# A first product by seven products in place of eight, with its sums formed in two PSUM banks

## The chip, the cores and the metric

One core of a Trainium2 chip runs one program. The metric is the time of one execution on the device in microseconds; the median of several runs is compared. The engines are named as the profile names them: PE is TensorE (PEld its weight loads), DVE is VectorE, ACT is ScalarE, POOL is GpSimd, and SP is SyncE, which issues most DMAs.

## The reference, cut to what matters

With S = 2048 rows, D = 576 columns and 4608 hidden features:

```
xn = layernorm(q)                                  # over the 576 columns
ks = causal convolution of k over 4 rows, per column
y  = causal convolution of (ks * v) over all 2048 rows, per column, by FFT
     + ks * v * ssm_D
h  = max(xn @ w1, 0)                               # 2048 x 576 by 576 x 4608: "first product"
out = q + xn * y + h @ w2                          # 2048 x 4608 by 4608 x 576: "second product"
```

All of it is in float32. The kernel keeps that precision on TensorE by splitting each operand into a high and a low part in the type fp32r and adding three matmuls (high by high, high by low, low by high); the product of two low parts is left out.

## The kernel before, in words

The 2048 rows are 16 tiles of 128, or 4 blocks of 512 rows (`BT` = 4 tiles each). The blocks are done in two halves of two blocks, because the running sums `acc` of one half (8 tiles of 576 columns) fill the space there is. In each half the 4608 features go by in 12 chunks of 384 (`FT` = 3 feature tiles of 128).

For a chunk and a block, `mm1` (L324 to L342) computes each feature tile transposed, 128 features by 512 rows, in one PSUM bank of the pool `ps_h` (2 banks): the 576 columns of x are four contraction tiles of 128 with three matmuls each (`h1` by `hi`, `h1` by `lo`, `l1` by `hi`), and a fifth of 64, whose high and low part lie stacked in one tile (`hl`), with two. That is 14 matmuls of 512 columns at L334. ScalarE then writes the high part `hh` of the relu (L339) and VectorE the low part `ll` (L340); both read the bank, and the bank is free after them. Those are the weights of the second product: `mm2` (L346 to L380) makes 128 rows by 288 columns in a bank of `ps_o` (3 banks) with 3 feature tiles x 3 = 9 matmuls of 288 columns (L358), and VectorE adds it to `acc` (L362 for the first block, which still multiplies by `rstd`, L366 for the others).

The weights arrive by DMA on SP (`load_w1`, L282; `load_w2`, L294). ScalarE makes the high part (`h` at L306 and L315) and GpSimd subtracts for the low part (`split_lo`, L277). `first_xT` (L211) and `make_xT` (L246) normalise a block's rows, transpose them on TensorE (L234, L269) and split them (`xhi` at L203 on ScalarE, `xlo` at L204 on VectorE). Blocks 2 and 3 are made so at the end of the first half.

The long convolution is a second stream of work, the generator `conv` (L410 to L714), in four stages: `fk` transforms the kernel `ssm_k` (loaded as `kt`, L421), `fx` forms and transforms `ks * v` (matmuls at L398), `fm` multiplies in the transformed domain (matmuls at L562, with most of ScalarE's work), and `fo` transforms back (L700, L701). Its matmuls are 128 x 288 and go to three further banks, `ps_f`. `tick` (L726) decides when the stream's next step is issued: each piece of the feed-forward part passes its cost in matmul columns, a rate turns it into credit, and one step is taken when there is credit. Steps have weights `W_FK`, `W_FX`, `W_FM`, `W_FO` (L54), and a step may ask for a pause. `here` (L402) queues a step's ScalarE and VectorE instructions behind the latest relu and the latest addition to `acc`. The tool that builds the program orders each engine's queue by a model of the time line; on the chip each queue runs in that order.

Of the kernel before, what the change touches and what calls it, by code (L numbers as in the profile page):

```python
# [17 lines left out]
P = 128  # L18
# [8 lines left out]
FT = 3  # L27
FC = FT * P
NCHUNK = DFF // FC
# [15 lines left out]
W_MM1 = 14 * 512  # L45
W_MM2 = FT * 6 * NH
PAUSE = 16000
START = 4000
PAUSES = 16
SHARE = 0.985  # L50
# [3 lines left out]
W_FK, W_FX, W_FM, W_FO = 1.4, 4.1, 1.26, 2.4  # L54
KD = 36
KT_GAP = 6000
FFT_TOTAL = N_FK * W_FK + N_FX * W_FX + N_FM * W_FM + N_FO * W_FO

SPLITS = {(0, 1): ((1, 0),), (0, 2): ((1, 1),), (1, 0): ((1, 2), (2, 0)), (1, 1): ((2, 1),),
          (1, 2): ((2, 2),)}  # L60
SPLITS0 = {(1, 0): ((1, 0), (1, 1)), (1, 1): ((1, 2), (2, 0)), (1, 2): ((2, 1), (2, 2))}
FFN_TOTAL = NCHUNK * NB * (FT * W_MM1 + BT * W_MM2)


# [44 lines left out]
def h3_ffn_kernel(ctx: ExitStack, tc, x, k, v, shift_k, ssm_k, ssm_D, w1, w2, fwd, inv, mid, out):  # L109
# [8 lines left out]
    hp = ctx.enter_context(tc.tile_pool(name="hp", bufs=2 * FT))  # L118
    xp = ctx.enter_context(tc.tile_pool(name="xp", bufs=2))
    dram = ctx.enter_context(tc.tile_pool(name="dram", bufs=1, space=DRAM))  # L120
    ps_h = ctx.enter_context(tc.tile_pool(name="ps_h", bufs=2, space=PSUM))
# [11 lines left out]
    fin = dram.tile([HT // 2, P, 2, D], F32, name="fin")  # L133

# [21 lines left out]
    def load_x(t, tag, bufs, **queues):  # L156
        pair = xp.tile([P, 2, D], F32, tag=tag, name=f"{tag}{t}", bufs=bufs)
        move(pair, x, slice(t, t + 2), **queues)
        return pair

    def load_acc(t, **queues):
        pairs[t] = load_x(t, "acc", HT // 2, **queues)
        acc[t], acc[t + 1] = pairs[t][:, 0, :], pairs[t][:, 1, :]
# [27 lines left out]
    xT = {}  # L191
    done = {}

    def xT_tiles(b):
        hi = xp.tile([P, 4, 512], F32R, tag="xhi", name=f"xhi{b}")
        lo = xp.tile([P, 4, 512], F32R, tag="xlo", name=f"xlo{b}")
        hl = xp.tile([P, 512], F32R, tag="xhl", name=f"xhl{b}")
        xT[b] = (hi, lo, hl)

    def split_x(b, c, ps):  # L200
        hi, lo, hl = xT[b]
        if c < 4:
            last = nc.scalar.activation(hi[:, c, :], ps, AF.Copy)  # L203
            nc.vector.tensor_tensor(lo[:, c, :], ps, hi[:, c, :], OP.subtract)  # L204
            return last
        else:
            done["act"] = nc.scalar.activation(hl[:64, :], ps[:64, :], AF.Copy)
            done["dve"] = nc.vector.tensor_tensor(hl[64:, :], ps[:64, :], hl[:64, :],
                                                  OP.subtract)

    def first_xT(srcs):  # L211

        xT_tiles(0)
# [3 lines left out]
        neg = xp.tile([P, BT], F32, tag="neg", name="neg", bufs=1)  # L217
        behind = None
        for t in range(BT):
            if t % 2 == 0:  # L220
                pair = xp.tile([P, 2, D], F32, tag="xn", name=f"xn{t}", bufs=BT // 2)
# [14 lines left out]
        for c in range(5):  # L236
            last = split_x(0, c, ps[c])
            if c == 1:
                with tc.issue_after(last.ins):
                    split_w1(0, 1)  # L240
# [5 lines left out]
    def make_xT(b, srcs, in_place=False):  # L246

        xT_tiles(b)
        t0 = b * BT
        for t in range(t0, t0 + BT):  # L250
            at = done["acc"] if in_place else lows[2 * (t - t0) // BT]
            with tc.issue_after(at.ins):
                stats(t, srcs[t])
        with tc.issue_after(at.ins):
            inv_std(t0, BT)
        xn = []
        for t in range(t0, t0 + BT):
            if in_place:
                xn.append(srcs[t])
            else:  # L260
                if t % 2 == 0:
                    pair = xp.tile([P, 2, D], F32, tag="xn", name=f"xn{t}", bufs=BT // 2)
                xn.append(pair[:, t % 2, :])
            normalized(xn[-1], srcs[t], t)
        for c in range(5):
            w = min(P, D - c * P)
            ps = fft_psum()
            for i in range(BT):
                nc.tensor.transpose(ps[:w, i * P:(i + 1) * P], xn[i][:, c * P:c * P + w], ident)  # L269
            split_x(b, c, ps)  # L270

    def at_turn(ci):

        return tc.issue_after(done["act"].ins) if ci else nullcontext()
# [7 lines left out]
    def load_w1(ci):  # L282
        f0 = (ci % NCHUNK) * FC
        r1 = wp.tile([P, 5, FC], F32, tag="r1", name=f"r1_{ci}", bufs=1)
        for o, step in ((0, P), (P, FC - P)) if ci == 0 else ((0, FC),):
            f, to = slice(f0 + o, f0 + o + step), slice(o, o + step)
            queue = nc.gpsimd if step == P else nc.sync
# [3 lines left out]
        raw_w[1, ci] = r1  # L291
        weights[ci] = [[None, None, None, None] for _ in range(FT)]

    def load_w2(ci):  # L294
        f0 = (ci % NCHUNK) * FC
        r2 = wp.tile([P, FT, D], F32, tag="r2", name=f"r2_{ci}", bufs=1)
        nc.sync.dma_start(r2, w2[f0:f0 + FC, :].rearrange("(j p) d -> p j d", p=P))
        raw_w[2, ci] = r2

    def split_w1(ci, j):  # L300
        r1 = raw_w[1, ci]
        h1 = wp.tile([P, 5, P], F32R, tag="h1", name=f"h1_{ci}_{j}", bufs=2 * FT - 1)
        l1 = wp.tile([P, 5, P], F32R, tag="l1", name=f"l1_{ci}_{j}", bufs=2 * FT - 1)
        cols = slice(j * P, (j + 1) * P)
        with at_turn(ci):
            nc.scalar.activation(h1, r1[:, :, cols], AF.Copy)  # L306
# [538 lines left out]
```

## Time and profile before

| what | value |
|---|---|
| runs | 1083.4, 1084.87, 1086.86 us; median 1084.87 us |
| profiled execution: span from first to last instruction | 1084.4 us |
| mean granted TensorE clock in it | 0.997 |
| DMA | 150.79 MB, 139 GB/s on average |
| TensorE idle before its own instructions, longest cases | 2.51 us at 56.69 us; 2.22 us at 12.07 us |
| POOL's wait for ScalarE's high parts at L277 | 448.3 us for w1, 168.8 us for w2 |

The profile gives the profiled execution by its span; it has no other time of its own. A busy share is the time in which at least one instruction of an engine is recorded as running. Matmuls are pipelined and their ends are modelled, so TensorE's pace is read from the chain of waits in order of time, where a piece lasts until the next begins. In the groups, the number behind the first bar is the busy time in us and the mean ns of one; behind the second bar stands the idle time of the engine just before these instructions and who ended it.

### The profile page before, as it was taken

The numbers are of one execution on the slowest core, as the hardware profiler recorded it, in microseconds if no ns is written. First come the engines' busy times: TensorE is split into PE (matmuls) and PEld (weight loads), VectorE is DVE, ScalarE is ACT, GpSimd is POOL, SyncE is SP. The second block draws the span as 40 slices with busy tenths as digits, with TensorE's granted clock in tenths as the row PEclk, the third lists the DMA queues.
The fourth block names the chain that finished last, engine by engine and source line by source line (L and its number), as shares of the span: only waits on it lengthen the run. The fifth ranks groups of instructions, "written<-read, shape, count | busy, mean of one in ns | idle before, by whom it ended". The sixth has DMA issues, their size and how long they took to land.

```text
span 1084.4 us, 17301 instructions
## 1 busy us (share of the span) xinstructions
PE 1070.8 (99%) x6537; PEld 977.2 (90%) x6537; DVE 732.5 (68%) x1213; ACT 585.0 (54%) x1184; POOL 261.9 (24%) x218
## 2 busy tenths in 40 slices
PE   8999999999999999999999999999999999999998
PEld 5889899998999999999999999899999999999998
DVE  5423677949998777677666676666656666876774
ACT  4221587823443323333388787888788864543430
POOL 4131222412312322312213031211113032332410
PEclk9999999999999999999999999999999999999999
DMA  9950345664644525325564343434344227745524
GB/s 217 181 145 27 119 147 190 195 185 133 187 138 136 153 77 164 117 60 171 190 182 135 99 135 99 135 99 136 92 143 141 80 103 221 201 130 143 164 81 110
DMA packets 112255, 150.79 MB, mean 139 GB/s; under 512 B 45261, under 2 KB 62927, under 8 KB 112172
## 3 DMA queue, kind: packets, MB, share of 16 engines
q1 hardware_dynamic: 103884, 135.50, 42.0%
q0 software_dynamic: 7968, 13.44, 4.8%
q8 instruction: 52, 0.85, 0.3%
q10 hardware_dynamic: 320, 0.74, 0.3%
q14 instruction: 31, 0.25, 0.1%
HBM read 114.26 MB, written 35.39 MB: 138 GB/s over the span
## 4 chain that ended last, share of the span: by engine, by line
PE 90%; DMA 4%; SPq 2%; DVE 2%; ACT 1%; issue 1%; POOL 0%; ACTq 0%; DVEq 0%
PE pso L358 40%; PE psh L334 39%; PE psf L562 7%; PE psf L398 3%; DMA r<-in_w 3%; SPq L421 2%; PE psf L700 1%; PE psf L701 1%; DMA k-1_2414<-in_k 1%; DMA sk<-in_shift_k 0%; PE psf L269 0%; DVE lok L553 0%; POOL l L277 0%; DVE k L611 0%; DVE lox L553 0%
## 5 line engine op out<-in xcount | busy, mean ns | idle before, releaser
L277 POOL TENSOR_TENSOR l<-r,h 128x640 fp32r<-128x640 f32 (+1 forms) x144 | 224.4, 1563 | 621.8 <-ACT h L306 448.3
L358 PE MATMUL pso<-h,hh 128*128 128x288 f32 x1152 | 337.3, 295 | 3.7 <-ACT hh L339 2.7
L358 PE MATMUL pso<-l,hh 128*128 128x288 f32 x1152 | 338.5, 295 | 0.0
L358 PE MATMUL pso<-h,ll 128*128 128x288 f32 x1152 | 337.7, 295 | 0.0
L334 PE MATMUL psh<-xhi,h 128*128 128x512 f32 x576 | 226.5, 394 | 1.1 <-DVE ll L340 1.1
L334 PE MATMUL psh<-xlo,h 128*128 128x512 f32 x576 | 226.5, 393 | 0.0
L334 PE MATMUL psh<-xhi,l 128*128 128x512 f32 x576 | 225.8, 392 | 0.0
L358 PEld LDWEIGHTS pso<-h,hh 128*128 128x128 f32 x1152 | 215.8, 188 | 10.4 <-ACT hh L339 3.4
L358 PEld LDWEIGHTS pso<-l,hh 128*128 128x128 f32 x1152 | 216.3, 188 | 5.8
L358 PEld LDWEIGHTS pso<-h,ll 128*128 128x128 f32 x1152 | 216.0, 188 | 0.6
L366 DVE TENSOR_TENSOR acc<-pso,acc 128x288 f32<-128x288 f32 x288 | 128.6, 451 | 75.1 <-PE pso L358 72.1
L339 ACT ACTIVATE hh<-psh 128x512 fp32r<-128x512 f32 x144 | 85.6, 595 | 169.1 <-PE psh L334 168.2
L340 DVE SCALAR_TENSOR_TENSOR ll<-psh,hh 128x512 fp32r<-128x512 f32 x144 | 99.0, 687 | 109.8 <-ACT hh L339 109.5
L334 PEld LDWEIGHTS psh<-xhi,l 128*128 128x128 f32 x576 | 108.4, 188 | 20.3
L334 PEld LDWEIGHTS psh<-xhi,h 128*128 128x128 f32 x576 | 108.4, 188 | 17.1 <-DVE ll L340 1.4
L334 PEld LDWEIGHTS psh<-xlo,h 128*128 128x128 f32 x576 | 108.6, 188 | 15.5 <-DVE xlo L204 0.4
L315 ACT ACTIVATE h<-r 128x576 fp32r<-128x576 f32 x72 | 48.9, 682 | 73.4 <-DMA r<-in_w 46.9
L362 DVE SCALAR_TENSOR_TENSOR acc<-pso,rstd,acc 128x288 f32<-128x288 f32 x96 | 48.3, 512 | 27.5 <-PE pso L358 26.5
L392 DVE TENSOR_TENSOR ks<-kt,ks 64x288 fp32r<-64x288 f32 x64 | 57.6, 901 | 3.3 <-ACT ks L391 1.3
L399 ACT ACTIVATE zx<-psf 128x288 f32<-128x288 f32 x64 | 25.8, 407 | 59.3 <-PE psf L398 38.9
L334 PE MATMUL psh<-xhl,l 128*128 128x512 f32 x144 | 56.4, 392 | 0.0
L334 PE MATMUL psh<-xhl,h 128*128 128x512 f32 x144 | 56.2, 391 | 0.0
(109 smaller groups left out, 1451.2 us busy)
## 6 DMA issues: line engine op xcount, KB each, us to landing
r<-in_w SPq DMA_DIRECT2D x24, 864.0 KB, 5.3
r<-in_w SPq DMA_DIRECT2D x23, 768.0 KB, 6.1
zk<-zk SPq DMA_DIRECT2D x32, 288.0 KB, 2.5
zx<-zx SPq DMA_DIRECT2D x32, 288.0 KB, 2.6
ztk<-zk SPq DMA_DIRECT2D x32, 288.0 KB, 3.0
ztx<-zx SPq DMA_DIRECT2D x32, 288.0 KB, 2.8
zy<-vo SPq DMA_DIRECT2D x32, 288.0 KB, 2.1
zo<-zy SPq DMA_DIRECT2D x32, 288.0 KB, 3.0
```

Source lines behind the costliest of these rows:

```text
L277: return nc.gpsimd.tensor_tensor(dst, src, hi, OP.subtract)
L315: nc.scalar.activation(h2, r2[:, j, :], AF.Copy)
L334: nc.tensor.matmul(ps, a, m, start=i == 0, stop=i == len(seq) - 1)
L339: done["act"] = nc.scalar.activation(hh, ps, AF.Relu)
L340: lows.append(nc.vector.scalar_tensor_tensor(ll, ps, 0.0, hh, op0=OP.max, op1=OP.subtract))
L358: nc.tensor.matmul(ps[:, :NH], a[:, cols], m[:, dc], start=n == 0, stop=n == 3 * FT - 1)
L362: done["acc"] = nc.vector.scalar_tensor_tensor(acc[t][:, dc], ps[:, :NH], rstd[:, t:t + 1], acc[t][:, dc], op0=OP.mult, op1=OP.add)
L366: done["acc"] = nc.vector.tensor_tensor(acc[t][:, dc], ps[:, :NH], acc[t][:, dc], OP.add)
L392: nc.vector.tensor_tensor(dst[other], src[own], dst[own], OP.subtract)
L398: nc.tensor.matmul(ps[:, :NH], w[:, u, n, :], stk, start=n == 0, stop=n == 1)
L399: nc.scalar.activation(z, ps[:, :NH], AF.Copy)
L562: nc.tensor.matmul(ps[:, :NH], a, m[:, cols], start=n == 0, stop=n == 2)
```

## The change

**Feature tiles and work.** `FT` becomes 2; a "pair" n is 256 features, and there are 18 pairs in a half. The list `visits` goes through pairs and blocks so that the block visited last for one pair is visited first for the next (blocks s = 0, 1, then 1, 0, ...).

**The first product.** From the third pair on (68 of 72 visits) `quad` takes the place of `mm1`. It treats the two feature tiles, the four full contraction tiles (taken two and two) and the two row halves of the block (`HR` = 256 rows) as 2 x 2 matrices and makes the four results by 7 products in place of 8, each of 2 contraction tiles x 3 = 6 matmuls of 256 columns. The fifth contraction tile stays as it was (`rest`, 2 matmuls of 512 columns a feature tile). The pool `ps_h` still has two banks, now as `h0` and `h1`; the sums of products are formed in them by further matmuls, by two ScalarE copies (`m5`, and one from bank to bank) and by two VectorE adds that read a bank and `m5` and write a bank.

**The sums of operands.** GpSimd makes four sums of w1 tiles a pair (`sum_w`), and `split_group` splits the sums and the plain tiles, 2048 columns and the fifth tile's 256 a pair where 1280 were split. For the rows, `sums` makes `t1` to `t4` of a block on VectorE and splits them. All block sums are made before the convolution begins: those of blocks 0 and 1 (`keep_first`) during the third and fourth visit, those of blocks 2 and 3 (`later_xT`) during the first `quad` visits, stored in DRAM (`kept`) and loaded again (`fetch`) at the last pair of the first half.

**The second product.** Its work is cut into units of one row tile and 288 columns (`unit`), for the two pairs that a block has seen last, 12 matmuls a bank (6 where a block starts or ends with one pair). `fill` issues units worth two pairs after each of the four stages of a `quad`.

**The convolution.** Its stream starts after the block sums; constants come one tile at a time with 3 buffers; some tiles have fewer buffers; step weights become 1.73, 3.5, 1.94 and 2.2, the pause between pieces of `kt` 3000 columns in place of 6000, and the share of the feed-forward work over which it is spread 0.96 in place of 0.985.

```diff
-FT = 3
+FT = 2
+HR = 256
...
-W_FK, W_FX, W_FM, W_FO = 1.4, 4.1, 1.26, 2.4
+W_FK, W_FX, W_FM, W_FO = 1.73, 3.5, 1.94, 2.2
...
-KT_GAP = 6000
+KT_GAP = 3000
...
+    kept = dram.tile([HB, P, 4 * 7 * HR + 512], F32, name="kept")
...
+        with here():
+            tt(v[:, 0], b12, b11, OP.subtract)
+            split("t1", 0)
+        yield
+        with here():
+            tt(v[:, 2], high[:, :, b22], b12, OP.subtract)
+            tt(v[:, 2], low[:, :, b22], v[:, 2], OP.add)
+        yield
...
+    def sum_w(n, k):
...
+        dst, a, b, op = ((s13[:, :, left], one[:, :, right], two[:, :, right], OP.add),
+                         (s24[:, :, left], s13[:, :, left], one[:, :, left], OP.subtract),
+                         (s13[:, :, right], one[:, :, left], one[:, :, right], OP.subtract),
+                         (s24[:, :, right], two[:, :, left], s24[:, :, left], OP.subtract))[k]
+        nc.gpsimd.tensor_tensor(dst, a, b, op)
...
+    def product(n, s, a, b):
+        hi, lo = weights[n][a]
...
+        for kp in range(2):
+            seq += [(hi[:, kp], m[:, 0, kp]), (hi[:, kp], m[:, 1, kp]), (lo[:, kp], m[:, 0, kp])]
+        return seq
+
+    def quad(n, s, m):
+
+        first, other = slice(0, HR), slice(HR, 512)
+        pb, pa = bank(m, f"psb{n}_{s}"), bank(1 - m, f"psa{n}_{s}")
+        run_seq(pb[:, other], product(n, s, "s1", "t1"), True)
+        run_seq(pb[:, first], product(n, s, "a11", "b11"))
+        m5 = xp.tile([P, HR], F32, tag="m5", name=f"m5_{n}_{s}", bufs=1)
+        nc.scalar.activation(m5, pb[:, other], AF.Copy)
+        done["act"] = nc.scalar.activation(pa[:, first], pb[:, first], AF.Copy)
+        yield
+        run_seq(pa[:, first], product(n, s, "a12", "b21"))
+        run_seq(pb[:, first], product(n, s, "s2", "t2"))
+        nc.vector.tensor_tensor(pa[:, other], pb[:, first], m5, OP.add)
+        yield
+        run_seq(pb[:, first], product(n, s, "s3", "t3"))
+        nc.vector.tensor_tensor(pb[:, other], pb[:, first], m5, OP.add)
+        run_seq(pa[:, other], product(n, s, "s4", "b22"))
+        run_seq(pa, rest(n, 0, s))
+        relu(n, s, 0, pa)
+        yield
+        run_seq(pb[:, first], product(n, s, "a22", "t4"))
+        run_seq(pb, rest(n, 1, s))
+        relu(n, s, 1, pb)
+        yield
...
+    def fill():
+        room = 2
+        while work and work[0][0] <= room:
+            size, args = work.pop(0)
+            unit(*args)
+            room -= size
...
+            parts = quad(n, s, q % 2)
+            for st in range(4):
+                next(parts)
+                if n + 1 < HALVES * NPAIR:
+                    if second:
+                        split_group(n + 1, st)
+                        if st == 3 and n + 2 < HALVES * NPAIR:
+                            load_w1(n + 2)
+                    else:
+                        sum_w(n + 1, st)
+                if st == 1:
+                    split_w2(n, second)
+                    if n + 1 < HALVES * NPAIR:
+                        load_w2(n + 1, second)
...
+                tick(W_STAGE[st])
+                fill()
+                if n == NPAIR - 1:
+                    fetch(s, (("b11", "t1"), ("t2",), ("t3", "b2"), ("t4", "xr"))[st])
...
+        if second == 0:
+            phase([n] if m == 0 else [n - 1, n], s, b, last)
+        elif last:
+            phase([n], s, b, True)
```

603 lines of the change are left out of this document (400 added, 203 removed).

## The prediction, made before the change was run

> **What bounds the kernel now.** I read the page first, then the chain of waits in order of time for the pace of TensorE, then the groups by line and form for the price of each operation, and last the waits.
>
> ```profile
> span 1084.4 us, 17301 instructions
> PE 1070.8 (99%) x6537; PEld 977.2 (90%) x6537; DVE 732.5 (68%) x1213; ACT 585.0 (54%) x1184; POOL 261.9 (24%) x218
> ...
> ACT  4221587823443323333388787888788864543430
> ...
> PEclk9999999999999999999999999999999999999999
> ...
> PE 90%; DMA 4%; SPq 2%; DVE 2%; ACT 1%; issue 1%; POOL 0%; ACTq 0%; DVEq 0%
> ```
> ```profile
> 97.01 3.19 PE psh L334 x14
> 100.20 2.38 PE pso L358 x18
> ```
> ```profile
> L358 PE MATMUL pso<-h,hh 128*128 128x288 f32 x1152 | 337.3, 295 | 3.7 <-ACT hh L339 2.7 <-DVE acc L366 0.9
> L334 PE MATMUL psh<-xhi,h 128*128 128x512 f32 x576 | 226.5, 394 | 1.1 <-DVE ll L340 1.1
> L334 PEld LDWEIGHTS psh<-xhi,h 128*128 128x128 f32 x576 | 108.4, 188 | 17.1 <-DVE ll L340 1.4 <-ACT xhi L203 0.3
> L334 PE MATMUL psh<-xhl,h 128*128 128x512 f32 x144 | 56.2, 391 | 0.0
> ```
>
> TensorE is at work all the time, at full clock, and the chain is 90% TensorE. Its busy time overlaps itself (one 512-column matmul is down for 394 ns, yet 14 pass in 3.19 us), so I price by pace: 512 columns take 3.19/14 = 228 ns, 288 columns 2.38/18 = 132.3 ns. The first product has 3x576 + 2x144 = 2016 matmuls of 512 columns, 460 us; the second 3x1152 = 3456 of 288 columns, 457 us; the remaining 167 us are the convolution's matmuls, the start, the end and waits. What makes TensorE's stream shorter comes off the end, as long as nothing new stops it.
>
> **The first product.** A block of 512 rows and a pair of feature tiles took 2x12 matmuls of 512 columns on the first four contraction tiles (24 x 228 = 5472 ns) plus 4 on the fifth. After, 7 products of 2 contraction tiles x 3 terms are 42 matmuls of 256 columns; the 4 stay. No 256-column matmul stands in the trace. On the line through the two paces, (228 - 132.3)/224 = 0.427 ns a column, 256 columns take 118.6 ns: 42 x 118.6 = 4981 ns, 491 ns saved. Bounds: half of 228 is 114 (saving 684 ns), and a matmul of 288 columns with a weight load of the same form takes 132.3 (5557 ns, a loss of 85 ns). I take 118.6, next to the near row. Four of the 72 visits stay plain, so 68 x 491 ns = **-33.4 us** (bounds -46.5 and +5.8).
>
> The Trainium skill, "TensorE: Matmul & The Clock Gate", Back-to-back issue gap, gives N/2.4 + 2.5 ns for a warm matmul: 216 and 109 ns, an estimated saving of 593 ns a visit, 40 us in all. The trace's 228 is above its 216, so the row decides.
>
> **Second product and convolution.** The same 3456 matmuls of 288 columns, grouped 12 or 6 to a bank in place of 9, and the same convolution: 0 on TensorE. Evictions fall from 384 to 304 (38 phases of 8).
>
> **The other engines.**
>
> ```profile
> L366 DVE TENSOR_TENSOR acc<-pso,acc 128x288 f32<-128x288 f32 x288 | 128.6, 451 | 75.1 <-PE pso L358 72.1
> L277 POOL TENSOR_TENSOR l<-r,h 128x640 fp32r<-128x640 f32 x72 | 116.5, 1619 | 452.8 <-ACT h L306 448.3 <-PE psf L562 4.5
> ...
> L277 POOL TENSOR_TENSOR l<-r,h 128x576 fp32r<-128x576 f32 x72 | 108.0, 1506 | 169.0 <-ACT h L315 168.8
> ...
> L340 DVE SCALAR_TENSOR_TENSOR ll<-psh,hh 128x512 fp32r<-128x512 f32 x144 | 99.0, 687 | 109.8 <-ACT hh L339 109.5
> L339 ACT ACTIVATE hh<-psh 128x512 fp32r<-128x512 f32 x144 | 85.6, 595 | 169.1 <-PE psh L334 168.2
> ...
> L306 ACT ACTIVATE h<-r 128x640 fp32r<-128x640 f32 x72 | 52.6, 732 | 4.5 <-DMA r<-in_w 4.0
> ...
> L362 DVE SCALAR_TENSOR_TENSOR acc<-pso,rstd,acc 128x288 f32<-128x288 f32 x96 | 48.3, 512 | 27.5 <-PE pso L358 26.5
> ...
> L399 ACT ACTIVATE zk<-psf 128x288 f32<-128x288 f32 x64 | 25.5, 401 | 13.5 <-PE psf L398 8.5 <-DMA zk<-zk 3.0 <-PE psh L334 1.3
> ```
>
> ScalarE: two copies of 256 columns a visit; from 401 (288) and 595 (512) about 375 ns each, 68 x 0.75 = 51 us; splits of w1 per pair 3 x 0.6 + 2 x 0.38 for 2 x 0.73, 34 x 1.1 = 37 us; block sums 4 x 6 x 0.6 = 14 us: 585 becomes 687. VectorE: two adds out of a bank a visit at about 0.42 us (451 for 288), +57 us; 80 evictions fewer, -38; block sums 4 x 10 x 0.75 = +30: 781. GpSimd: (1619 - 1506)/64 = 1.77 ns an element, so 512 take 1.39 and 256 take 0.94 us; a pair's w1 now needs 3 x 1.39 + 2 x 0.94 for splits and 4 x 0.94 for sums, 9.8 us in place of 3.2: 34 x 6.6 = +224, 486. Over some 1060 us that is 65, 74 and 46%. None of the three binds on average, and a pair's weights have two visits (some 27 us) to be made in.
>
> ```profile
> 543.34 2.83 POOL L277 TENSOR_TENSOR l<-r,h 128x576 fp32r<-128x576 f32 x2 [3.20 <-ACT h L315]
> ```
> ```profile
> 544.39 0.45 DVE L366 TENSOR_TENSOR acc<-pso,acc 128x288 f32<-128x288 f32 x1
> 544.93 1.85 DVE L553 TENSOR_TENSOR lox<-ztx,hix 128x576 fp32r<-128x576 f32 x1
> ...
> 547.07 0.74 DVE L553 TENSOR_TENSOR lok<-ztk,hik 128x576 fp32r<-128x576 f32 x1
> ```
> ```profile
> 600.00:760.00 160.00, 158.68 (x998) 146.69 (x997) 105.28 (x173) 129.78 (x288) 29.57 (x18) 1.00 0.37 116
> ```
>
> Two things sharpen it. GpSimd subtracts from 543.34 to 546.17: VectorE's add out of a bank at 544.39 keeps its 0.45 us, but the subtract at 544.93, both inputs in SBUF, takes 1.85 us and ends just behind GpSimd; the same operation takes 0.74 at 547.07. (The Trainium skill, "GPSIMD Engine Reference", Key points, says that GpSimd shares its SBUF interfaces with VectorE, with contention where two inputs lie in SBUF; the trace agrees.) The new adds read a bank and are spared, but with GpSimd busy almost twice as long what queues ahead of them is late more often. And the transform's middle stage (600 to 760 us) has ScalarE at 129.8 of 160 us. The new weights give that stage 372 of 848 shares in place of 242 of 748, so its own ScalarE work thins out to about three quarters while the first product's grows: I expect 80 to 90% there again.
>
> **The new waits.** This is the term I know least. A visit now has TensorE wait on the two banks it is still adding into. After stage 1 ScalarE copies twice (m5, then the other bank) before stage 2 may begin; after stage 2 VectorE adds once before stage 3. Behind the waiting matmul the whole TensorE queue stands. The cover is the fill: 12 matmuls, 12 x 132.3 = 1.59 us. The needs are about 0.2 (a matmul is recorded as ending 394 - 228 ns after the next has begun) + 0.75 = 0.95 us, and 0.2 + 0.42 = 0.62 us, so 0.64 and 0.97 us are left over for an engine that comes late. Stage 3 to 4 and one visit to the next have over 2.7 us of cover. How late the two engines come:
>
> ```profile
> ACT hh L339 <- PE psh L334: 168.2, 83, 7.4
> DVE ll L340 <- ACT hh L339: 109.5, 79, 9.8
> DVE acc L366 <- PE pso L358: 72.1, 88, 3.9
> ```
> ```profile
> 300.15 0.40 PE L334 MATMUL psh<-xhl,l 128*128 128x512 f32 x1
> ...
> 302.32 1.40 ACT L391 ACTIVATE xs<-c 64x576 fp32r<-64x576 f32 x2 [4.50 <-DVE c L492]
> ...
> 303.74 0.60 ACT L339 ACTIVATE hh<-psh 128x512 fp32r<-128x512 f32 x1
> ```
>
> In 83 of 144 cases ScalarE stood ready when the bank was full, so 61 (42%) came late; VectorE was ready for 79 of 144 and 88 of 288. The operation that stands ahead is mostly one of the rows above, 0.4 to 0.9 us, and half of it is left on average: the margin covers that. The timeline shows a bad case: the bank full at 300.55, ScalarE held 4.50 us by VectorE, the eviction at 303.74, 3.2 us late. Today two banks and a whole visit absorb this; after, it would stop TensorE for 3.2 - 0.64 = 2.6 us. Of 2 x 68 = 136 tight boundaries, if 42% are late, a quarter of these beyond the margin, and those by 0.9 us: 136 x 0.42 x 0.25 x 0.9 = **+13 us**. Bounds: 0 (all covered), and 57 us (every late one over by 1 us).
>
> **Start and middle.**
>
> ```profile
> 14.29 0.79 PE L334 MATMUL psh<-xhi,h 128*128 128x512 f32 x1
> ...
> 30.27 2.02 PE L269 MATMUL psf<-ident,xn 128*128 128x128 f32 x12
> ...
> 56.69 0.61 PE L358 MATMUL pso<-h,hh 128*128 128x288 f32 x1 [2.51 <-ACT hh L339]
> ```
> ```profile
> 32.88 1.28 DVE L204 TENSOR_TENSOR xlo<-psf,xhi 128x512 fp32r<-128x512 f32 x2
> ```
> ```profile
> ACT h L315 <- DMA r<-in_w: 46.9, 15, 8.8
> ```
> ```profile
> 480.00:600.00 120.00, 120.00 (x751) 110.59 (x750) 80.17 (x155) 69.78 (x146) 27.64 (x19) 1.00 0.53 163
> ```
>
> The first visit has two feature tiles where it had three: 28 matmuls of the first product and 8 units of 6 of the second, 28 x 0.228 + 48 x 0.132 = 12.7 us of work from 14.3, plus 2 us of transposes, lasts to 29. The second block's first tiles are split by about 33 (32.88 + 1.28 for two), so some 4 us are bare. Against that, the convolution's kernel loads move behind the block sums, and the 2.5 us at 56.69, when a w2 split waited for its load, should go: **+2 us** net (0 to +5). In the middle the sums of two blocks, 7680 words a partition or 3.9 MB each, come back from DRAM within two visits (27 us), 146 GB/s; at 480 to 600 us 163 GB/s took 0.53 of the DMA engines, which leaves 145: **+2 us** (0 to +8).
>
> **Sum.** 1084.4 - 33.4 + 13 + 2 + 2 = **1068.0 us**. The page gives the profiled execution by its span; the median of the runs, 1084.87, stands 0.5 above it, which I leave out.
>
> **Rivals.** *Everything is covered* and the narrow matmul pays: 1084.4 - 33.4 + 2 = 1053 (1046 with some of the 114 ns pace). For it: more than half of the evictions began at once. 0.23.
>
> *The banks decide*, slower: TensorE stands at stage 2 behind ScalarE's second copy. It turns the gain when the 136 boundaries cost over 29.4 us, 0.22 us each. If half the late ones pass the margin by 1.3 us (the middle of 0 and 2.6): 136 x 0.42 x 0.5 x 1.3 = 37 us, 1084.4 - 33.4 + 37 + 4 = 1092. For it: the 3.2 us case and a busier GpSimd; against: TensorE that stands lets the others catch up. 0.20. The Trainium skill, "Perfetto Trace Analysis", Optimizing Tensor Performance, speaks for it: groups should rotate through banks so that the eviction of one overlaps the next, and larger matmuls beat smaller ones. By that rule the banks read in mid-sum are the loss; the trace bears it out only for late cases, since the fill lies between.
>
> *The weight load decides*: 256 columns run no faster than 288 at 132.3 ns, so the first product gets 5.8 us longer: 1084.4 + 5.8 + 17 = 1107. For it: each load is down for 188 ns, and there are 46 a visit in place of 28. Against: 188 ns already overlaps itself at a pace of 132.3. 0.06. A pace of 125 would save only 68 x 222 ns = 15 us, 1086, no change.
>
> **Numbers.** Forecast (1060 to 1081) 0.47; covered 0.23; banks 0.20; weight load 0.06; a little of several, about 1085, 0.04. A measurement tells 0.3% (3.3 us) from nothing. Faster 0.47 + 0.23 = 0.70; same 0.04 + 0.03 of the banks + 0.02 of the weight load (the pace of 125) = 0.09; slower the rest, 0.21. The range runs from 1046 (covered, good pace) to 1098 (banks).
>
> **What would show it.** Right: 42-matmul visits at 115 to 121 ns, TensorE's idle time before the stage 2 and 3 matmuls under 20 us together, released by the ScalarE copy and the VectorE add; GpSimd near 450 us. Wrong: a 256-column pace over 125 ns, or idle time of TensorE over 30 us, most in the middle stage; or a convolution that ends after the last first-product visit, so that the tail holds more than the second product.

## The result and the profile after

The changed kernel takes 1130.03 us (median of four runs, 1127.61 to 1131.58), beside 1085.86 us for the kernel before in the same series. The ratio is 1.0403 [1.0378, 1.0427]: slower by 4%, where 1068.0 us and a range up to 1098 had been forecast.

The page of the kernel after, first its span and engine totals, then VectorE's and GpSimd's busy tenths and the granted clock in 40 slices of 28 us, then the chain that ended last:

```profile
span 1128.1 us, 21092 instructions
...
PE 1067.1 (95%) x7761; PEld 1025.5 (91%) x7761; DVE 803.6 (71%) x1309; ACT 668.3 (59%) x1454; POOL 489.6 (43%) x492
...
DVE  5578733677759999888466667676576665589985
...
POOL 3243444455435444564433344433343443545541
PEclk9998998999998999998999999999999999999999
...
PE 67%; DVE 17%; DMA 5%; SPq 4%; issue 3%; ACT 3%; POOL 1%; POOLq 0%; DVEq 0%; ACTq 0%
```

The chain was 90% TensorE and 2% VectorE; now it is 67% and 17%. The averages say little: VectorE at 71% looks free. The slices say more. From the 13th to the 16th, 340 to 450 us, VectorE's digit is 9. That is the convolution's input stage `fx`, which runs from 343 to 546 us (first to last matmul that reads `xs`). Before, it ran from 261 to 533.

The same stage by windows, first of the kernel before, then of the kernel after, with a steady stretch of the middle stage below it. The columns are PE, PEld, DVE, ACT and POOL busy in us (with instruction counts), granted clock, DMA share and GB/s:

```profile
260.00:360.00 100.00, 100.00 (x610) 91.61 (x609) 89.86 (x132) 38.43 (x72) 24.05 (x20) 1.00 0.48 145
```
```profile
345.00:445.00 100.00, 85.36 (x594) 80.88 (x594) 95.55 (x126) 41.85 (x89) 50.14 (x47) 0.95 0.55 157
...
760.00:860.00 100.00, 100.00 (x762) 98.65 (x761) 67.33 (x111) 82.63 (x191) 40.87 (x36) 1.00 0.38 116
```

In the input stage VectorE is busy for 95.55 of 100 us, GpSimd for 50 in place of 24, and TensorE has dropped to 85.36. In the middle stage, which the prediction feared for its ScalarE (82.63), TensorE is never idle.

To add up what TensorE loses, I take from the trace the time from the start of each matmul to the start of the next and subtract the median of that shape. The sum of what is left is called **lost time** here, and the rest of the span the stall-free stream. Lost time counts waits and also matmuls that run slowly behind a wait.

| lost time, us, by time in the run | 0–100 | 100–300 | 300–600 | 600–1000 | 1000–end | sum |
|---|---|---|---|---|---|---|
| before | 13.5 | 2.7 | 1.4 | 4.4 | 0.4 | 22.4 |
| after | 22.4 | 13.0 | 43.2 | 5.2 | 7.2 | 91.0 |

The stall-free stream is 1084.4 - 22.4 = 1062.0 us before and 1128.1 - 91.0 = 1037.1 after. So the change did shorten TensorE's work, by 24.9 us, and gave back 68.6 us in lost time, 41.8 of them between 300 and 600 us: 1084.4 - 24.9 + 68.6 = 1128.1.

Who ended TensorE's waits in the kernel after (total us, times, longest):

```profile
PE psb L525 <- DVE psa L574: 14.1, 9, 4.5
PE pso L606 <- DVE acc L610: 6.9, 4, 4.1
PE psb L525 <- DVE ll L532: 6.9, 5, 4.6
PE psb L525 <- DVE psb L577: 5.1, 3, 3.0
```

These four lead the list, and all are VectorE. L574 and L577 are the new adds in the banks, but `acc` and `ll` are old operations with the old buffers behind them, and they are late too. ScalarE's copies, which the prediction put first among the new waits, ended no wait of TensorE over 0.15 us.

One such wait in time order. TensorE, VectorE and GpSimd of the kernel after (start, duration; x6 covers six matmuls):

```profile
381.68 0.87 PE L525 MATMUL psa<-b,g 128*128 128x256 f32 x6
382.39 0.88 PE L525 MATMUL psb<-t,g 128*128 128x256 f32 x6
383.11 0.42 PE L656 MATMUL psf<-xs,wx 128*128 128x288 f32 x2
388.02 1.65 PE L525 MATMUL psb<-t,g 128*128 128x256 f32 x6 [4.49 <-DVE psa L574]
389.46 1.48 PE L525 MATMUL psa<-b,g 128*128 128x256 f32 x6
390.75 0.71 PE L525 MATMUL psa<-xr,g 128*128 128x512 f32 x2
```
```profile
382.10 1.87 DVE L745 TENSOR_TENSOR e<-k,sk 128x576 f32<-128x576 f32 x1
384.00 1.16 DVE L746 TENSOR_TENSOR c<-c,e 128x576 f32<-128x576 f32 x1
385.20 1.16 DVE L751 TENSOR_TENSOR c<-c,v 128x576 f32<-128x576 f32 x1
386.28 1.34 DVE L745 TENSOR_TENSOR e<-k,sk 128x576 f32<-128x576 f32 x1
387.55 0.42 DVE L574 TENSOR_TENSOR psa<-psb,m 128x256 f32<-128x256 f32 x1
```
```profile
381.44 1.91 POOL L424 TENSOR_TENSOR w<-r,w 128x576 fp32r<-128x576 f32 x1 [1.79 <-ACT w L511]
383.44 2.31 POOL L478 TENSOR_TENSOR r<-r 128x256 f32<-128x256 f32 x2
385.69 0.55 POOL L643 DMA_DIRECT2D wx<-in_fwd  x1
386.26 1.95 POOL L478 TENSOR_TENSOR r<-r 128x256 f32<-128x256 f32 x2
```

The reader is to see four things. Six matmuls of 256 columns take 382.39 - 381.68 = 0.71 us when nothing is in the way, 118 ns each, as forecast. The bank is full at about 383.3, but its add runs at 387.55, because four operations of the convolution's input stage stand ahead of it in VectorE's queue. Those four have both inputs in SBUF and take 5.5 us together while GpSimd computes beside them; the add itself, out of a bank, takes 0.42. And between the second and third stage of this visit TensorE has only two matmuls of the convolution to do, not twelve of the second product.

### The profile page after: what moved, and what is told of

Same layout as the page of the kernel before. It is cut to its first block, busy times and chain, and to the rows that moved or that the text cites. A ratio compares the mean times of both kernels' runs of the same rounds, so it can differ in the third digit from the quotient of the medians.

```text
span 1128.1 us, 21092 instructions
## 1 busy us (share of the span) xinstructions
PE 1067.1 (95%) x7761; PEld 1025.5 (91%) x7761; DVE 803.6 (71%) x1309; ACT 668.3 (59%) x1454; POOL 489.6 (43%) x492
## 4 chain that ended last, share of the span: by engine, by line
PE 67%; DVE 17%; DMA 5%; SPq 4%; issue 3%; ACT 3%; POOL 1%; POOLq 0%; DVEq 0%; ACTq 0%
PE pso L606 28%; PE psb L525 18%; PE psa L525 8%; PE psf L824 6%; DVE e L745 3%; SPq L679 3%; PE psh L525 2%; DVE c L746 2%; PE psf L656 2%; DMA r<-in_w 1%; DVE xs L650 1%; DVE ll L532 1%; DVE acc L614 1%; DVE acc L610 1%; DVE c L751 1%
## 5 line engine op out<-in xcount | busy, mean ns | idle before, releaser
L606 PE MATMUL pso<-w,hh 128*128 128x288 f32 x2304 | 469.9, 298 | 11.0 <-DVE acc L610 6.9
L606 PEld LDWEIGHTS pso<-w,hh 128*128 128x128 f32 x2304 | 371.6, 190 | 20.9 <-DVE acc L610 7.8
L424 POOL TENSOR_TENSOR g<-r,g 128x512 fp32r<-128x512 f32 (+2 forms) x178 | 207.4, 1174 | 379.2 <-ACT g L453 297.4
L606 PE MATMUL pso<-w,ll 128*128 128x288 f32 x1152 | 320.8, 297 | 3.9 <-DVE ll L532 3.9
L525 PE MATMUL psb<-t,g 128*128 128x256 f32 x1632 | 248.2, 287 | 26.2 <-DVE psa L574 14.1
L525 PEld LDWEIGHTS psb<-t,g 128*128 128x128 f32 x1632 | 220.3, 191 | 33.7 <-DVE psa L574 16.7
L606 PEld LDWEIGHTS pso<-w,ll 128*128 128x128 f32 x1152 | 211.3, 190 | 6.5 <-DVE ll L532 4.8
L424 POOL TENSOR_TENSOR w<-r,w 128x576 fp32r<-128x576 f32 x72 | 114.6, 1593 | 73.1 <-ACT w L511 72.9
L478 POOL TENSOR_TENSOR r<-r 128x256 f32<-128x256 f32 x136 | 115.6, 868 | 62.2 <-DMA r<-in_w 59.8
L525 PE MATMUL psa<-b,g 128*128 128x256 f32 x816 | 122.1, 286 | 0.0
L453 ACT ACTIVATE g<-r 128x512 fp32r<-128x512 f32 (+2 forms) x178 | 91.2, 535 | 29.3 <-POOL r L478 12.1
L532 DVE SCALAR_TENSOR_TENSOR ll<-psb,hh 128x512 fp32r<-128x512 f32 x68 | 46.6, 686 | 29.1 <-ACT hh L531 28.7
L650 DVE TENSOR_TENSOR ks<-kt,ks 64x288 fp32r<-64x288 f32 x64 | 54.4, 849 | 17.3 <-ACT ks L649 15.7
L610 DVE SCALAR_TENSOR_TENSOR acc<-pso,rstd,acc 128x288 f32<-128x288 f32 x80 | 39.4, 511 | 19.7 <-PE pso L606 19.1
```

The costliest lines, as they stand in the source:

```text
L424: return nc.gpsimd.tensor_tensor(dst, src, hi, OP.subtract)
L453: nc.scalar.activation(hi, src, AF.Copy)
L478: nc.gpsimd.tensor_tensor(dst, a, b, op)
L525: nc.tensor.matmul(ps, a, m, start=start and i == 0, stop=i == len(seq) - 1, skip_group_check=not start)
L532: lows.append(nc.vector.scalar_tensor_tensor(ll, ps, 0.0, hh, op0=OP.max, op1=OP.subtract))
L606: nc.tensor.matmul(ps[:, :NH], a, m, start=i == 0, stop=i == len(seq) - 1)
```

## The experiments

Three theories were set against each other. A: the new step weights and the later start pack the convolution's stages too densely. B: the waits in the middle of a visit, on banks that are still being summed, cost by themselves. C: GpSimd's doubled work holds off VectorE's operations with two inputs in SBUF, so that whatever waits for VectorE is late.

### The step weights (theory A)

In `e1_weights` the kernel after gets more evenly spread stages:

```diff
-W_FK, W_FX, W_FM, W_FO = 1.73, 3.5, 1.94, 2.2
+W_FK, W_FX, W_FM, W_FO = 1.78, 4.2, 1.82, 2.8
```

> The changed kernel with one edit: the weights of the four convolution stages, 1.73, 3.5, 1.94, 2.2, become 1.78, 4.2, 1.82, 2.8, so that the input stage (fx) and the output stage (fo) are spread over more of the run and the middle stage (fm) over less. Theory A (VectorE is full in the input stage, 95.5 of 100 us at 340 to 440 us, and everything that waits for it there stops TensorE): the input stage grows from 203 to about 235 us, VectorE falls under 90% there, TensorE's lost time between 300 and 600 us falls by half and more, the run takes 1098 to 1112 us. Theory B (the sums in the two banks stop TensorE wherever they stand, because VectorE and ScalarE answer too late for the cover of 1.59 us): the number of waits stays, 1122 to 1134 us.

Measured: 1142.65 us, ratio 1.0527 [1.0493, 1.0561], slower still and outside both forecasts. The input stage became 21 us longer (345 to 569 us), but its lost time stayed (45.9 us between 300 and 600), and 600 to 1000 us now loses 15.2 in place of 5.2. VectorE is still busy for 92.71 of the 100 us from 345 to 445, where under 90 had been expected.

In `e5_before_weights` the kernel before gets the step weights of the kernel after:

```diff
-W_FK, W_FX, W_FM, W_FO = 1.4, 4.1, 1.26, 2.4
+W_FK, W_FX, W_FM, W_FO = 1.73, 3.5, 1.94, 2.2
```

> The kernel before with the changed kernel's weights of the four convolution stages (1.73, 3.5, 1.94, 2.2 for 1.4, 4.1, 1.26, 2.4) and nothing else. Its input stage gets shorter, from 273 to about 225 us. If VectorE's density alone stops TensorE (theory A without the new waits): 1095 to 1115 us. If it takes the tight waits of the new first product to turn a late VectorE into lost time: 1082 to 1090 us.

Measured: 1084.55 us, ratio 0.9999 [0.9981, 1.0017]. Its input stage lasts only from 259 to 455 us, denser than in the kernel after, and the run loses 1.5 us between 300 and 600. Its first 100 us, in the columns of the windows above:

```profile
259.00:359.00 100.00, 100.00 (x611) 91.69 (x611) 93.90 (x138) 40.80 (x78) 25.80 (x21) 1.00 0.53 156
```

VectorE is at 93.90 of 100 us and TensorE never idle. Density alone does not stop TensorE: theory A falls.

### GpSimd taken away, then added (theory C)

`e2_no_wsums` takes out the sums of w1 tiles on GpSimd; the splits read plain tiles.

```diff
-        nc.gpsimd.tensor_tensor(dst, a, b, op)
...
-            split_into(n, four[0], four[1], pairs_[:, :, 0:4:2, left])
+            split_into(n, four[0], four[1], r1[:, 0:4, left].rearrange("p (t r) f -> p t r f", t=2))
...
```

> The changed kernel without GpSimd's four sums of w1 tiles per pair; the splits take plain tiles in their place, so the first product is another one. GpSimd loses 136 operations of 868 ns, 118 us of 490, and ScalarE's splits no longer wait for GpSimd. Theory C (GpSimd holds up VectorE's operations on two SBUF inputs, and that is what makes VectorE late): those operations get shorter, VectorE's share in the input stage falls from 95 to under 90%, 1095 to 1112 us. Theory A without C (the convolution's own work is too dense there): 1118 to 1128 us. Theory B: 1125 to 1132 us.

Measured: 1116.57 us, ratio 1.0298 [1.0264, 1.0332]; lost time 76.2 us, 39.2 of it between 300 and 600. GpSimd goes from 489.6 to 376.4 us. The edit takes away every wait of ScalarE for a sum of GpSimd's (12.1 us in three cases in the kernel after), so those waits were not the main part of the loss. The time lies just under the range of theory A and above that of theory C, whose sign does not appear either: VectorE is busy for 97.12 of the 100 us from 338 to 438, and its total falls only from 803.6 to 788.2. This run alone does not speak for C.

`e7_pool_silent` takes out the low parts as well, and TensorE uses the high part in their place, with the same matmuls:

```diff
-        split_lo(lo, src, hi)
...
-        nc.gpsimd.tensor_tensor(dst, a, b, op)
...
-            seq += [(hi[:, kp], m[:, 0, kp]), (hi[:, kp], m[:, 1, kp]), (lo[:, kp], m[:, 0, kp])]
+            seq += [(hi[:, kp], m[:, 0, kp]), (hi[:, kp], m[:, 1, kp]), (hi[:, kp], m[:, 0, kp])]
...
```

> The changed kernel with GpSimd left with its DMA issues alone: no sums of w1 tiles and no low parts of w1 and w2 (the high part stands in for the low one, so both products are others; TensorE's matmuls are as many and as long). Theory C (GpSimd holds up VectorE's operations on two SBUF inputs): the convolution's 160 VectorE operations of the input stage fall from 975 ns on average to 750 to 780 ns, TensorE's lost time between 300 and 600 us falls from 43 to under 15 us, 1072 to 1092 us. Theory A alone (the stage is too dense for VectorE even undisturbed): the operations get shorter but half the loss stays, 1098 to 1112 us.

Measured: 1075.69 us, ratio 0.9912 [0.9892, 0.9931], 0.9% under the kernel before; lost time 41.5 us, 13.1 of it between 300 and 600. Its engine totals, and the first 100 us of its input stage:

```profile
PE 1049.9 (97%) x7761; PEld 1017.8 (94%) x7761; DVE 706.4 (66%) x1309; ACT 667.4 (62%) x1454; POOL 54.2 (5%) x106
```
```profile
334.00:434.00 100.00, 99.14 (x742) 95.60 (x741) 90.98 (x149) 51.21 (x114) 10.58 (x20) 1.00 0.67 192
```

GpSimd's 54.2 us are almost all DMA issues. VectorE executes the same 1309 instructions as in the kernel after and needs 706.4 us in place of 803.6. It is still busy for 90.98 of 100 us in this stage, and TensorE for 99.14. The place in the trace that corresponds to the wait shown above, on VectorE:

```profile
367.12 0.75 DVE L741 TENSOR_TENSOR e<-k,sk 128x576 f32<-128x576 f32 x1
367.91 0.76 DVE L742 TENSOR_TENSOR c<-c,e 128x576 f32<-128x576 f32 x1
368.69 1.54 DVE L646 TENSOR_TENSOR xs<-c,xs 64x576 fp32r<-64x576 f32 x2
370.26 0.76 DVE L741 TENSOR_TENSOR e<-k,sk 128x576 f32<-128x576 f32 x1
370.94 0.42 DVE L570 TENSOR_TENSOR psa<-psb,m 128x256 f32<-128x256 f32 x1
```

A queue much like it stands ahead of the same add, but an operation of 128x576 takes 0.75 us, and TensorE loses 0.6 us at this boundary in place of 4.65. A part of that difference is cover: TensorE has eight matmuls of the convolution to do here in place of two, 0.8 us more.

`e11_before_pool` goes the other way. The kernel before, with the step weights of the kernel after (harmless by `e5_before_weights`), makes each low part of w1 three times on GpSimd. Nothing reads the two extra copies, and no wait on a bank is added:

```diff
         split_lo(l1, r1[:, :, cols], h1)
+        for n in range(2):
+            more = wp.tile([P, 5, P], F32R, tag="more", name=f"more{ci}_{j}_{n}", bufs=1)
+            split_lo(more, r1[:, :, cols], h1)
```

> The kernel before with the changed kernel's stage weights and with GpSimd's subtract for each w1 tile made three times (two results unused), so that GpSimd is busy for about 490 us as in the changed kernel. If a GpSimd that holds up VectorE costs time by itself: 1105 us and above. If it takes the new first product's short waits on top: 1082 to 1094 us.

Measured: 1139.65 us, ratio 1.0501 [1.0474, 1.0529], 55 us slower than the kernel before; lost time 71.8 us, 33.2 of it between 300 and 600. Its engine totals, the first 100 us of its input stage, and who ended TensorE's longest waits:

```profile
PE 1088.9 (96%) x6537; PEld 986.1 (87%) x6537; DVE 818.3 (72%) x1213; ACT 582.0 (51%) x1184; POOL 528.0 (46%) x362
```
```profile
264.00:364.00 100.00, 89.72 (x521) 80.50 (x520) 94.24 (x116) 33.59 (x65) 49.30 (x32) 0.97 0.43 135
```
```profile
PE pso L361 <- DVE acc L369: 16.2, 7, 4.0
PE pso L361 <- DVE acc L365: 5.5, 8, 1.4
```

VectorE's 1213 instructions, the same as before, now take 818.3 in place of 732.5 us, and TensorE waits for the additions to `acc`; GpSimd itself ended only 0.2 us of the waits of its matmuls. The groups by line and form show which operations grew. Kernel before, kernel after, `e7_pool_silent`, `e11_before_pool` (the last figure before the second bar is the mean ns of one):

```profile
L487 DVE TENSOR_TENSOR c<-c,e 128x576 f32<-128x576 f32 x48 | 39.6, 825 | 1.3
...
L492 DVE TENSOR_TENSOR c<-c,v 128x576 f32<-128x576 f32 x16 | 14.7, 916 | 0.2
```
```profile
L614 DVE TENSOR_TENSOR acc<-pso,acc 128x288 f32<-128x288 f32 x224 | 96.7, 450 | 57.7 <-PE pso L606 56.9
...
L746 DVE TENSOR_TENSOR c<-c,e 128x576 f32<-128x576 f32 x48 | 42.1, 878 | 0.4
...
L751 DVE TENSOR_TENSOR c<-c,v 128x576 f32<-128x576 f32 x16 | 18.8, 1175 | 0.3
```
```profile
L610 DVE TENSOR_TENSOR acc<-pso,acc 128x288 f32<-128x288 f32 x224 | 97.3, 451 | 66.1 <-PE pso L602 65.0
...
L742 DVE TENSOR_TENSOR c<-c,e 128x576 f32<-128x576 f32 x48 | 36.1, 752 | 0.5
...
L747 DVE TENSOR_TENSOR c<-c,v 128x576 f32<-128x576 f32 x16 | 12.0, 752 | 0.2
```
```profile
L369 DVE TENSOR_TENSOR acc<-pso,acc 128x288 f32<-128x288 f32 x288 | 127.3, 451 | 55.3 <-PE pso L361 53.2
L490 DVE TENSOR_TENSOR c<-c,e 128x576 f32<-128x576 f32 x48 | 59.2, 1233 | 0.9
...
L495 DVE TENSOR_TENSOR c<-c,v 128x576 f32<-128x576 f32 x16 | 21.1, 1316 | 0.3
```

With GpSimd almost silent an operation of 128x576 with both inputs in SBUF takes 752 ns; the means rise with GpSimd's work to 825 and 916 (262 us of GpSimd), 878 and 1175 (490 us), 1233 and 1316 (528 us). GpSimd's share alone does not set the mean: the kernel after and `e11_before_pool` have GpSimd busy for 50.14 and 49.30 of 100 us in their input stages, and `c<-c,e` at 878 and 1233. The addition out of a bank stays at 450 or 451 ns in all of them. The Trainium skill, "GPSIMD Engine Reference", Key points, names VectorE's instructions with two SBUF inputs among those in contention with GpSimd; the rows agree.

### The waits in the banks (theory B)

Both kernels without the convolution's stream, so that VectorE has only the work of the products:

```diff
 def begin_stream():
-        clock["done"] = False
...
-    rest_of_stream()
```

> The changed kernel without the convolution's stream (the output lacks xn * y). TensorE's work free of waits was 1037 us in the changed kernel, and the convolution's matmuls are 960 x 132.3 ns = 127 us of it: 910 us stay. Theories A and C: without the convolution VectorE has room, the waits of the input stage go, 920 to 940 us, and less than the kernel before without it. Theory B: the waits in the banks stay, 950 to 970 us, no less than the kernel before without it.

> The kernel before without the convolution's stream (the output lacks xn * y): 1084.4 - 127 = 957 us; every theory expects 950 to 962 us.

Measured: 937.44 us after, 953.94 us before. Here the change is worth 16.5 us. The kernel after loses 23.1 us in its first 100 us, 3.0 in the next 200, and 0.9 in all the rest.

```profile
PE 915.6 (98%) x6801; PEld 887.0 (95%) x6801; DVE 355.1 (38%) x728; ACT 283.9 (30%) x590; POOL 392.3 (42%) x395
```

GpSimd still works for 392 us, and every wait in the banks is still there. With VectorE at 38% (and ScalarE at 30%) neither costs more than that after 300 us. Theory B falls as it was stated: the waits are a place where lateness becomes visible, not its source.

`e9_fills` is meant to give more cover to the wait behind the second stage and less to the end of the visit:

```diff
-                fill()
+                for _ in range((1, 2, 1, 0)[st]):
+                    fill()
```

> The changed kernel with the same four fills a visit placed otherwise: 1, 2, 1, 0 units of work after stages 1 to 4 in place of 1, 1, 1, 1. The first VectorE add is covered by 3.2 us in place of 1.59. If VectorE is late in bursts of up to 3 us: 1108 to 1120 us. If VectorE is full in that stage, so that more cover is only used up: 1124 to 1134 us.

Measured: 1128.26 us, ratio 1.0404 [1.0383, 1.0425], no change; lost time 91.9 us. The part that ends with the add L574 fell from 15.7 to 8.2 us, the part that ends with `ll` of the first tile rose from 7.7 to about 12, and the part that ends with `xs` from 2.8 to 10.7. But in the trace the edit hardly adds the cover that it names: between the second and third stage, the seven visits with the least cover in the input stage have 6, 0, 6, 0, 6, 6 and 0 matmuls of the second product, 24 together where the kernel after has 27 (66 and 57 with the convolution's own), and these boundaries lose 18.0 us in place of 16.9. So the run says that moving the waits does not remove the loss; what full cover would do it leaves untested.

`e3_no_adds` leaves out VectorE's two adds of a visit, and ScalarE copies the whole bank in their place:

```diff
-        done["act"] = nc.scalar.activation(pa[:, first], pb[:, first], AF.Copy)
+        done["act"] = nc.scalar.activation(pa, pb, AF.Copy)
...
-        nc.vector.tensor_tensor(pa[:, other], pb[:, first], m5, OP.add)
...
-        nc.vector.tensor_tensor(pb[:, other], pb[:, first], m5, OP.add)
```

> The changed kernel without VectorE's two adds in the banks (they are left out, and ScalarE's copy from bank to bank takes all 512 columns, so the first product is another one). TensorE no longer waits for VectorE inside a visit, only for ScalarE after stage 1 and for the relu between visits. In the changed kernel the waits that these adds end are 22 us, and the half-speed matmuls behind the long ones about 8 us more. If these waits are the place where a late VectorE costs time: 1092 to 1106 us. If VectorE's lateness goes through whatever TensorE needs next from it (low parts of the relu, sums into acc): 1108 to 1122 us, with the waits for those grown.

Measured: 1095.23 us, ratio 1.0092 [1.0069, 1.0115]; lost time 56.3 us, 26.4 of it between 300 and 600. It takes away 57.6 us of VectorE's work (28.9 + 28.7) as well as the two waits, so it cannot say which of the two helped. VectorE's total falls by 19 us only, to 784.7: its operations with two SBUF inputs got longer still (`c<-c,e` 1016 ns in place of 878). What is left waits for `ll`, 13.8 us in eight cases.

### VectorE's own share, and the loads

`e8_no_taps` takes work off VectorE's queue where it is full: taps 1 to 3 of the short convolution are left out.

```diff
...
-                        nc.vector.tensor_tensor(e, win[t - n], sk[:, n, :], OP.mult)
-                        nc.vector.tensor_tensor(sums[t], sums[t], e, OP.add)
```

> The changed kernel without taps 1 to 3 of the short convolution (the output has only the first of four taps): 96 VectorE operations on two SBUF inputs fewer in the input stage, about 95 us of VectorE. Theories A and C (VectorE's lateness in the input stage is the loss): the lost time between 300 and 600 us falls from 43 to under 10 us, 1082 to 1094 us. Theory B (waits in the banks whatever VectorE does besides): above 1110 us.

Measured: 1095.62 us, ratio 1.0098 [1.007, 1.0126]; lost time 56.1 us, and 13.1 between 300 and 600, the same as with GpSimd silent. Both are a little above the forecast (under 10 us, and 1094). GpSimd still works for 476 us. So most of the loss between 300 and 600 us needs both: a queue of VectorE that is full in that stage, and a GpSimd that lengthens it.

`e6_kt_gap` sets the pause between pieces of the convolution's kernel back to that of the kernel before:

```diff
-KT_GAP = 3000
+KT_GAP = 6000
```

> The changed kernel with the pause between the pieces of the convolution's kernel load at 6000 columns as before, in place of 3000. The changed kernel loses 4.7 us and about 3 us of half-speed matmuls after it at 182 us, where ScalarE stands 10.6 us behind GpSimd's sum, which waits for w1 behind those loads. If that is the cause, this wait goes and the run takes 1118 to 1126 us; but the stream also starts its first stage later, by about 20 us, and is then denser everywhere: if that weighs more, 1130 to 1140 us.

Measured: 1120.53 us, ratio 1.0334 [1.0303, 1.0365]; lost time 82.4 us, counted with 216 ns for the 25 warm-up matmuls as in the kernel after (over half of them ran at half pace in this run, and their own median would hide it). The time is the forecast one, but not for the forecast reason: TensorE still waits 4.3 us at 188 us, and the first 300 us lose 34.3 in place of 35.4. What shrinks lies behind 600 us, 4.5 in place of 12.4, and why is open. This is a smaller cost of its own, about 10 us; the input stage keeps its loss (43.5 us between 300 and 600).

### Seven products only where there is room

`e10_second_half` uses the plain product through the first half, where the input stage lies, and seven products in the second (36 visits). The sums of blocks 0 and 1 are not made, and some buffers, loads and fills are placed anew with it.

```diff
-FFN_TOTAL = 4 * W_PLAIN + (4 * NPAIR - 4) * W_QUAD + 4 * NPAIR * 4 * W_UNIT
+FFN_TOTAL = 2 * NPAIR * W_PLAIN + 2 * NPAIR * W_QUAD + 4 * NPAIR * 4 * W_UNIT
...
+        elif n < NPAIR:
+            for j in range(FT):
+                mm1(n, s, j)
```

> The changed kernel with the seven products in the second half of the rows alone (36 visits in place of 68); the first half keeps the plain product of 14 matmuls of 512 columns a feature tile, and no block sums of blocks 0 and 1 are made. The convolution's input stage then lies beside the plain product with GpSimd at its old load, and the middle stage, where the changed kernel loses nothing (100% of 100 us at 760 to 860 us), beside the seven products. If the account is right: 36 x about 0.4 us gained, the loss at 300 to 600 us under 8 us, 1066 to 1078 us. If the loss comes with the regrouping (pairs of tiles, the late start of the stream): 1085 to 1110 us.

Measured: 1089.17 us, ratio 1.0044 [1.0029, 1.0059], 0.4% above the kernel before. The 1066 to 1078 us that the account had forecast were missed, and the time lies in the range of the other reading. Most of the loss has gone (28.6 us, 12.2 of it between 300 and 600, where under 8 had been expected), but so has most of the gain: the stall-free stream is 1086.1 - 28.6 = 1057.5 us, 4.5 less than before. By the medians of its shapes, 256 columns run here at 120 ns, so a visit saves 24 x 228 - 42 x 120 = 432 ns, 36 visits 15.6 us; the 1152 matmuls of 512 columns run at 231 ns in place of 228 (+3.5), the 4416 of 288 columns at 133 in place of 132 (+4.4), and from the start of the last matmul to the end it takes 7.4 us in place of 4.3 (+3.2, an end that the stream holds too). That leaves the 4.5. Of the kernels that compute the whole reference none beat the kernel before beyond what can be told apart.

## Why the prediction was wrong

**The matmuls: right.** The pace of 256 columns was taken as 118.6 ns and is 119. A visit saves 24 x 228 - 42 x 119 = 474 ns where 491 was forecast, 32.2 us over 68 visits; the matmuls of 512 columns that stay run at 232 ns, so the first product as a whole gained 30.7 us beside the -33.4. The second product, set at 0, costs 3.5 us (133 ns in place of 132), the convolution's matmuls 1.0, and the stretch from the start of the last matmul to the end got 1.4 us longer. So the stream got shorter by 24.9 us. The weight load as rival is out.

**The totals of the other engines: right, and no help.** 687, 781 and 486 us were forecast for ScalarE, VectorE and GpSimd (the last paragraph of the prediction has 450 for GpSimd); 668, 804 and 490 were measured. The step that failed is the sentence drawn from them, "None of the three binds on average". It divided by the whole run. VectorE was already full in the input stage of the kernel before, 89.86 of 100 us in the window above. The row of VectorE's slices, which the prediction leaves out of the page, has three 9s there (244 to 325 us), and over the 100 us around the start of that stage VectorE is busy for 91.64:

```profile
DVE  5423677949998777677666676666656666876774
```
```profile
240.00:340.00 100.00, 99.06 (x600) 90.25 (x599) 91.64 (x130) 37.47 (x69) 30.82 (x23) 1.00 0.53 162
```

What the change adds to VectorE and GpSimd falls on that stage as on every other.

**GpSimd's hold: seen, and priced at nothing.** The prediction showed the subtract that took 1.85 us beside GpSimd and 0.74 without, and concluded that the new adds read a bank and are spared. They are: 0.42 us. But they stand in one queue behind operations that are not. VectorE's total says what that was worth: 803.6 - 706.4 = 97 us over the run by `e7_pool_silent`, for 489.6 - 54.2 = 435 us of GpSimd's work, about 0.22 us for each. In the kernel before it is 85.8 for 266.1, 0.32 (`e11_before_pool`). `e2_no_wsums` gives less, 15.4 for 113.2, 0.14.

**The new waits: +13 us forecast, +68.6 of lost time in all measured**, where start and middle had 4 more. Three premises of that term did not hold. The cover, "12 matmuls, 12 x 132.3 = 1.59 us", isn't there at each boundary: counted in the trace, the second-product matmuls between the second and the third stage are 0, 0, 6, 6, 0, 6 and 9 in the visits at 347, 383, 418, 452, 484, 512 and 546 us, and 25 to 36 in the six visits between them. What stands ahead in the wait shown above is not one operation of which half is left, but four. And the lateness was read from averages over the run (61 of 144 late) and spread evenly over 136 boundaries, whereas most of it lies in one stage: 41.8 of the 68.6 us. ScalarE's second copy, the wait that the rival *the banks decide* named, ended no wait of TensorE over 0.15 us. That rival had the sign, but 1092 us, the wrong engine and the wrong stage, so what it got right is luck.

**Start and middle.** The start was set at +2; the first 100 us lose 8.9 us more than before, and the next 200 another 10.3. The fetch of the stored sums, set at +2, cost nothing: TensorE is busy for all 55 us from 540 to 595, at a DMA share of 0.98 and 331 GB/s. That is more than the prediction had in mind, whose 146 GB/s holds one block of 3.9 MB in 27 us; two are 291 GB/s.

**What is shown and what is not.** That GpSimd's work is the cause of most of the loss is shown from both sides: without it 49.5 of the 68.6 us go and the change gains 0.9% (`e7_pool_silent`), and with it the old kernel slows down by about as much, with none of the new waits (`e11_before_pool`). The other 19.1 us stay with GpSimd silent and have other causes. That it needs a full VectorE queue is shown by `e4_after_no_conv` and `e8_no_taps`. How the loss divides between the thin cover and the hold is open. In the kernel after, the seven thin boundaries lose 16.9 us and the six with 25 to 36 matmuls 3.1, with GpSimd at work beside both; `e7_pool_silent` has boundaries just as thin (0, 0, 0, 6, 0, 0 and 9 in the same visits' places) and loses 2.6 us there; and no run had cover at every boundary and a busy GpSimd. The causes of the losses in the first 300 us were not separated either.

## What to carry to other kernels

Read each engine's share in the stage where it is highest, not over the run, before work is added to it: an engine at 68% of the span was at 90% of 100 us, and there the change was paid for. The share is a warning and not a price: at 93.90 and 90.98 of 100 us with little work on GpSimd, VectorE cost TensorE next to nothing (`e5_before_weights`, `e7_pool_silent`). Work given to GpSimd is also paid on VectorE, here 0.1 to 0.3 us for each us of operations on SBUF, by everything that waits in VectorE's queue, whether or not the waiting operation itself is held. Count the cover at each boundary in the queue's real order; a fill that the code issues at a point may run elsewhere.

## What the runs showed of the hardware

The hold reaches VectorE's operations with two SBUF inputs: the mean of `c<-c,v` went from 752 ns with GpSimd silent to 1316, while additions that read a bank stayed at 450 or 451 ns in four kernels. It is not confined to them. The normalisation `xn<-xn,mv,rstd` of 128x576, with one large input, takes about 575 ns with GpSimd silent, but 1681 and 1679 ns at 497.94 and 500.04 us of the kernel before and 1823 ns at 575.12 us of `e11_before_pool`. Each of the three began during a subtract of GpSimd and ended 0.3 us behind it.

A wait of a few microseconds costs more than itself. After the 4.49 us shown above, the next two groups of six matmuls took 1.44 and 1.29 us from start to start, beside 0.71 before the wait. The granted clock is 0.51 from 388 to 391 us, where it is 0.95 over the window from 345 to 445. Matmuls at such a clock, the waits themselves left out, make up 7.5 of the 43.2 us lost between 300 and 600 us. The Trainium skill, "TensorE: Matmul & The Clock Gate", Part 1, has the clock fall to half after an idle window of about 3.4 us and come back after as long a busy one; the halving agrees, and here the doubled pace ended at about 391 us, 2.9 us after TensorE's start. A shorter wait than 3.4 us did it too: in the kernel before, the granted clock is 0.50 from 57 to 59.5 us, behind the wait of 2.51 us at 56.69.
